# Load and fold steps of x, the order of S1 and S2, and the setup's order in a Fourier-filter-and-MLP kernel

## The chip, the cores and the metric

The kernel runs on one core of a Trainium2 chip. The metric is the device time of one execution in microseconds (us). TensorE is called PE, its weight loads PEld, VectorE is DVE, ScalarE is ACT, GpSimd is POOL or Pool, SyncE is SP; "SPq" is a transfer issued by SyncE. "Granted clock" is TensorE's clock as the profile records it, as a share of full speed.

## The reference

```python
def _attn_ref(x, filt_r, filt_i):            # x: (8, 3072, 256)
    X = np.fft.rfft(x, axis=1)
    Y = X * (filt_r + 1j * filt_i)[None, :, :]
    return np.fft.irfft(Y, n=x.shape[1], axis=1).astype(np.float32)

def _moe_ref(x, w1, w2, w_out):              # x: (24576, 256), w1, w2: (256, 1024)
    return (np.maximum(x @ w1, x @ w2) @ w_out).astype(np.float32)
```

A filter in the frequency domain along the sequence, then a maxout MLP. The FFTs are done as matmuls in stages: S1 (x times a cosine table), S2 and the multiply by the filter, S3, S4.

The names in the profiles: x lands as `xf` and is folded into `xd` (sum and difference of its halves), which S1 reads. S1's result `pa` is copied to `at`, written to DRAM as `ad` and read back as `bt` for S2 (`px`); the multiply by the filter gives `pq`, S3 gives `pz`, copied to `zt`, written to DRAM as `zd` and read back as `zr` for S4 (`py`). `ph` and `po` belong to the MLP, `ot` is the output tile. The p-tiles lie in PSUM, the memory of the matmuls' results, until another engine copies them out. In the setup, "spreads" lay out the filter by matmuls and copies, T1 are transposes for batch 0, and dummy matmuls have results that nobody uses. A "hole" is a stretch of some microseconds in which PE stands.

## The kernel before

One main loop runs over 48 output tiles of 8 steps each. Each step has two matmuls into `ph` (`moe_h`) and five into `po` (`moe_o`); the S1, S2 and S3 work of later batches is hung on certain steps by a list ("plan"). Batch b's S2 and S3 are a generator with eight groups; S1 of batch b+1 rides in six of them. Transfers of x, `ad`, `bt`, `zd` and `zr` are issued by SyncE; output tiles are stored by Pool, which also folds x.

```python
    def load_p(b, c):                        # x as fp32, two transfers of 256 KB
        ...
        for m in range(2):
            ...
            nc.sync.dma_start(out=xb[b, c][64 * m:64 * m + 64], in_=...)

    def fold_x(b, c):                        # Pool: sum and difference
        xf = xb[b, c]
        xb[b, c] = xpool.tile([128, 2, 2 * D], BF16, tag="xb", name="xd")
        for i, op in enumerate((OP.add, OP.subtract)):
            G.tensor_tensor(xb[b, c][:, i], xf[:, 0], xf[:, 1], op)
...
        for j, g in enumerate((4, 5, 6, 7, 2, 3, 1, 0)):           # one group
            px = [ps.tile(...) for _ in range(2)]
            ...                                                    # S2: 8 matmuls into px
            for k in range(2):
                V.tensor_tensor(pq[k][0:FROWS], px[k]..., F[...], OP.mult)
            if b + 1 < B and j in (0, 1, 3, 4, 6, 7):
                f1_half(b + 1, (0, 1, 3, 4, 6, 7).index(j))        # S1 of the next batch
            ...                                                    # S3 of the group before
...
        if j % 4 == 3:                                             # in moe_o
            V.tensor_copy(ot[tt][:, n - 1:n + 1], po[tt])
        if j == 7 ...:
            G.dma_start(out=dst[:, 4 * i:4 * i + 4], in_=ot[tt])   # store, Pool's queue
...
    opool = ctx.enter_context(tc.tile_pool(name="opool", bufs=2))
```

Of the kernel before, what the change touches and what calls it, by code (L numbers as in the profile page):

```python
# [13 lines left out]
B = 8  # L14
# [15 lines left out]
def kernel(  # L30
# [26 lines left out]
    V, S, G, TE = nc.vector, nc.scalar, nc.gpsimd, nc.tensor  # L57
# [30 lines left out]
    def bank2(shape, dtype, name, tag=None):  # L88
        if tag is None:
            ring.append(ring.pop(0))  # L90
            tag = ring[-1]
        return p2.tile(shape, dtype, tag=tag, name=name)
# [27 lines left out]
    def expand_f(g, ri, E, sp=0):  # L120
        if E is V:
            pf = [p2.tile([128, 2, D], FP32, tag="px", name="pf", bufs=4) for _ in range(2)]
        else:
            p_ = bank2([128, 2, 2, D], FP32, "pf")
            pf = [p_[:, b] for b in range(2)]
        fs = Fs[ri]
        spin(pf[0].rearrange("p u d -> p (u d)"), sp)
        for b in range(2):
            for c in range(2):
                m = 4 * b + c  # L130
                TE.matmul(pf[b][64 * c:64 * c + 32], Sel[:, m], fs[:, 2 * g:2 * g + 2], start=True, stop=True)
                p0 = 64 * c + 32
                if g:
                    TE.matmul(pf[b][p0:p0 + 32], Sel[:, 7 - m], fs[:, 16 - 2 * g:14 - 2 * g:-1], start=True, stop=True)
                else:
                    TE.matmul(pf[b][p0:p0 + 32, 0], Sel[:, 7 - m + c], fs[:, 0], start=True, stop=True)
                    TE.matmul(pf[b][p0:p0 + 32, 1], Sel[:, 7 - m], fs[:, 15], start=True, stop=True)
        f_ = F[:, ri, :, 2 * g:2 * g + 2].rearrange("p b u d -> p b (u d)")
        if E is V:
            for b in range(2):  # L140
                V.tensor_copy(f_[:, b], pf[b].rearrange("p u d -> p (u d)"))
        else:
            evac(E, f_, p_.rearrange("p b u d -> p b (u d)"))
# [142 lines left out]
    def table_e(t1):  # L286
        V.tensor_scalar(t1, pid, 12.0, None, OP.is_equal)
        V.tensor_scalar(e0[:, 0:1], pid, 0.0, t1, OP.is_equal, OP.add)
        V.tensor_scalar(e0[:, 1:2], e0[:, 0:1], -1.0, 1.0, OP.mult, OP.add)
        V.tensor_scalar(e0[:, 0:1], e0[:, 0:1], -0.5, 1.0, OP.mult, OP.add)  # L290
# [45 lines left out]
    def spin(pd, n):  # L336
        for _ in range(n):
            TE.matmul(pd, Sp, Sp.rearrange("p (o x) -> p o x", o=1).to_broadcast([128, 4, 128]), start=True, stop=True)
# [65 lines left out]
    def f1_half(b, c):  # L404
        if c == 0:
            ad[b] = dram.tile([128, N2, D], BF16, tag="ad", name="ad")
        at = apool.tile([128, 4, D], BF16, tag="at", name="at")
        pa = [ps.tile([128, 2, D], FP32, tag="ps", name="pa") for _ in range(2)]
        for m, i in QUADS:
            TE.matmul(pa[m][64 * i:64 * i + 64], C1[64 * m:64 * m + 64, 64 * i:64 * i + 64],  # L410
                      xb[b, c][64 * m:64 * m + 64, i], start=True, stop=True)
        for m in range(2):
            S.activation(at[:, 2 * m:2 * m + 2], pa[m], AF.Copy)  # L413
        nc.sync.dma_start(out=ad[b][:, 4 * c:4 * c + 4], in_=at)
# [17 lines left out]
    def gen_f2(b):  # L432
        bt_ = bt[b]
        zd[b] = dram.tile([T, 96, D], BF16, tag="zd", name="zd")
        pend = []
        zt = None

        def s3(g, pq):
            nonlocal zt
            if zt is None:  # L440
                zt = zpool.tile([128, 2, 4, D], BF16, tag="zt", name="zt")
                made.clear()
            pz = [ps.tile([128, 2, D], FP32, tag="ps", name="pz") for _ in range(2)]
            for i in range(2):
                for ri, W in enumerate((VP, VQ)):
                    for c, k in QUADS:
                        TE.matmul(pz[c][64 * k:64 * k + 64, i], W[64 * c:64 * c + 56, 2 * g + i, k],  # L447
                                  pq[k][64 * c:64 * c + 56, ri, i], start=(ri == 0), stop=(ri == 1))
            o = 2 * (g % 2)
            for c in range(2):  # L450
                S.activation(zt[0:ROWS, c, o:o + 2], pz[c][0:ROWS], AF.Copy)  # L451
            made.append(g)
            if len(made) == 2:
                t0 = 8 * (g // 2)
                for k in range(2):
                    nc.sync.dma_start(out=zd[b][t0:t0 + 8, 48 * k:48 * k + 48].rearrange("t p d -> p t d"),
                                      in_=zt[64 * k:64 * k + 48].rearrange("p c u d -> p (c u) d"))
                zt = None

        made = []  # L460
        for j, g in enumerate((4, 5, 6, 7, 2, 3, 1, 0)):
            px = [ps.tile([128, 2, D], FP32, tag="ps", name="px") for _ in range(2)]
            for i in range(2):
                for k, c in QUADS:
                    t_ = 16 * i + 4 * (g // 2) + 2 * c + g % 2
                    TE.matmul(px[k][64 * c:64 * c + 64, i], U[64 * k:64 * k + 48, 4 * g + 2 * i + c],  # L466
                              bt_[64 * k:64 * k + 48, t_], start=True, stop=True)
            pq = []
            for k in range(2):
                pq.append(pqpool.tile([128, 2, 2, D], BF16, tag="pq", name="pq"))  # L470
                V.tensor_tensor(pq[k][0:FROWS],  # L471
                                px[k][0:FROWS].rearrange("p (o i) d -> p o i d", o=1).to_broadcast([FROWS, 2, 2, D]),
                                F[0:FROWS, :, k, 2 * g:2 * g + 2], OP.mult)
            if b + 1 < B and j in (0, 1, 3, 4, 6, 7):
                f1_half(b + 1, (0, 1, 3, 4, 6, 7).index(j))
            pend.append((g, pq))
            if len(pend) > 1:
                s3(*pend.pop(0))
            yield
        while pend:  # L480
            s3(*pend.pop(0))
        yield
# [15 lines left out]
    def first_t1(g, E):  # L498
        pt = p2.tile([128, 2, 2, D], BF16, tag="px", name="pt", bufs=4)
        t0 = 8 * (g // 2) + 2 * (g % 2)  # L500
        for c in range(2):
            for i in range(2):
                for dh in range(2):
                    TE.transpose(pt[:, c, i, 128 * dh:128 * dh + 128],
                                 At[:, 2 * dh:2 * dh + 2].rearrange("p b m t -> p t (b m)")[:, t0 + 4 * c + i], I128)
        o = bt[0][0:ROWS, 8 * (g // 2):8 * (g // 2) + 8].rearrange("p (c u) d -> p c u d", c=2)[:, :, 2 * (g % 2):2 * (g % 2) + 2]
        evac(E, o.rearrange("p c u d -> p c (u d)"), pt[0:ROWS].rearrange("p c u d -> p c (u d)"))

    def evac(E, out_, in_):
        if E is V:  # L510
            V.tensor_copy(out_, in_)
        else:
            S.activation(out_, in_, AF.Copy)
# [156 lines left out]
    load_f0()  # L670
    patch_f0()
    first_s1(5, S, 2)
    expand_f(1, 1, S)
    expand_f(6, 0, V)
    expand_f(7, 0, S, 2)
    first_t1(1, V)
    first_t1(2, V)
    table_e(t1)
    pend = []
    for n, g in enumerate(order):  # L680
# [41 lines left out]
    def plan(step, fn, *a):  # L722
        todo.setdefault(step, []).append((fn, a))

    def plan_x(n, steps):
        for c, s_ in enumerate(steps):
            plan(s_, load_p, n, c)
            plan(s_ + 5, fold_x, n, c)

    def plan_f2(n, steps, z1, z0):  # L730
        g = []
# [11 lines left out]
    def spaced(first, gap, count):  # L743
        return [first + int(gap * i) for i in range(count)]
# [4 lines left out]
        plan(int(0.6 * (c - 1)), f1, 1, c, (S, V)[c % 2])  # L749
    plan(6, f1_read, 1)  # L750
    plan_f2(1, spaced(17, 1.9, 9), 28, 34)
    plan_x(2, (5, 7, 8, 10, 11, 13))
    plan(36, f1_read, 2)
    plan_x(3, spaced(32, 3.5, 6))
    plan_f2(2, spaced(60, 2.5, 9), 74, 81)
    plan(83, f1_read, 3)
    plan_x(4, spaced(76, 3.5, 6))
    plan_f2(3, spaced(104, 3, 9), 121, 129)
    plan(130, f1_read, 4)
    plan_x(5, spaced(122, 3.5, 6))  # L760
    plan_f2(4, spaced(150, 3.3, 9), 168, 178)
    plan(179, f1_read, 5)
    for n in range(5, B):
        o = 48 * (n - 5)
        if n + 1 < B:
            plan_x(n + 1, spaced(168 + o, 3.5, 6))
            plan(227 + o, f1_read, n + 1)
        plan_f2(n, spaced(197 + o, 3.4, 9), 216 + o, 226 + o)

# [3 lines left out]
    for tt in range(6 * B + 1):  # L773
        b, i = divmod(tt, 6)
# [40 lines left out]
```

## Time and profile before

| | before |
|---|---|
| time, median of 2 runs | 579.49 us (578.09 to 580.88) |
| span of the profiled execution | 579.7 us |
| PE busy | 520.9 us, 90% |
| mean granted clock | 0.962 |
| chain that ended last | PE 62%, DMA 18%, ACT 5%, DVE 5% |

How to read it: PE is the bound wherever it has work, and the chain says that a fifth of the end's cause lies in transfers. Which transfers, and when, the page does not tell; the waits by engine and the equal stretches do. The prediction shows them. The DMA share of a stretch adds up the time of the packets that begin in it, over 16 engines, so it can pass 1.

### The profile page before, as it was taken

The numbers are of one execution on the slowest core, as the hardware profiler recorded it, in microseconds if no ns is written. First come the engines' busy times: TensorE is split into PE (matmuls) and PEld (weight loads), VectorE is DVE, ScalarE is ACT, GpSimd is POOL, SyncE is SP. The second block draws the span as 40 slices with busy tenths as digits, with TensorE's granted clock in tenths as the row PEclk, the third lists the DMA queues.
The fourth block names the chain that finished last, engine by engine and source line by source line (L and its number), as shares of the span: only waits on it lengthen the run. The fifth ranks groups of instructions, "written<-read, shape, count | busy, mean of one in ns | idle before, by whom it ended". The sixth has DMA issues, their size and how long they took to land.

```text
span 579.7 us, 12530 instructions
## 1 busy us (share of the span) xinstructions
PE 520.9 (90%) x5206; PEld 352.9 (61%) x5284; DVE 322.5 (56%) x437; ACT 337.2 (58%) x597; POOL 147.9 (26%) x168
## 2 busy tenths in 40 slices
PE   8898859995999969995999996999789999999997
PEld 3556536663566646673566763676456766677775
DVE  8887437431773446542775346745377368734442
ACT  7777538643686546853566563755456556655452
POOL 6681163126004070232405240051400000000000
PEclk9999979998799989998999997999979999999999
DMA  8982995898368954989449983789535873451102
GB/s 150 275 142 87 166 259 154 233 197 198 137 177 226 211 177 128 265 164 209 142 137 286 204 176 122 202 234 210 173 101 156 166 171 93 119 155 73 72 39 109
DMA packets 74093, 97.03 MB, mean 167 GB/s; under 512 B 5106, under 2 KB 49780, under 8 KB 73044
## 3 DMA queue, kind: packets, MB, share of 16 engines
q1 hardware_dynamic: 63012, 63.72, 49.6%
q0 software_dynamic: 11024, 32.51, 17.9%
q8 instruction: 41, 0.67, 0.5%
q14 instruction: 16, 0.13, 0.1%
HBM read 54.79 MB, written 47.19 MB: 176 GB/s over the span
## 4 chain that ended last, share of the span: by engine, by line
PE 62%; DMA 18%; ACT 5%; DVE 5%; SPq 4%; issue 3%; POOL 2%; POOLq 0%; DVEq 0%; ACTq 0%
PE po L620 22%; PE ph L595 20%; DMA xf<-in_x_dram 6%; DMA out_dram<-ot 5%; PE po L615 5%; SPq L423 3%; PE pz L447 3%; ACT at L413 3%; PE px L466 3%; DMA zd<-zt 2%; PE py L579 2%; POOL xd L402 2%; DVE pq L471 2%; DMA bt<-ad 2%; PE pa L410 2%
## 5 line engine op out<-in xcount | busy, mean ns | idle before, releaser
L600 ACT ACTIVATE gt<-ph 128x512 bf16<-128x512 f32 x308 | 181.6, 602 | 131.9 <-PE ph L595 131.3
L620 PE MATMUL po<-Wo,gt 128*128 128x256 bf16 x1536 | 234.5, 277 | 4.0 <-issue 0.7
L620 PEld LDWEIGHTS <-gt 128*128 128x128 bf16 x1536 | 152.6, 99 | 61.1 <-issue 3.3
L622 DVE COPY ot<-po 128x512 f32<-128x512 f32 x96 | 66.3, 690 | 156.2 <-PE po L620 106.2
L471 DVE TENSOR_TENSOR pq<-px,F 120x1024 bf16<-120x1024 f32 x112 | 131.7, 1219 | 30.6 <-PE px L466 29.7
L402 POOL TENSOR_TENSOR xd<-xf 128x512 bf16<-128x512 f32 x72 | 89.3, 1264 | 141.9 <-DMA xf<-in_x_dram 102.3
L627 POOL DMA_DIRECT2D out_dram<-ot x47 | 25.7, 548 | 271.8 <-DVE ot L622 271.8
L595 PEld LDWEIGHTS <-Wd 128*128 128x128 bf16 x768 | 71.5, 99 | 28.5 <-issue 19.8
L451 ACT ACTIVATE zt<-pz 112x512 bf16<-112x512 f32 x112 | 60.9, 600 | 26.1 <-PE pz L447 24.9
L413 ACT ACTIVATE at<-pa 128x512 bf16<-128x512 f32 x72 | 39.1, 595 | 57.8 <-PE pa L410 57.8
L598 DVE TENSOR_SCALAR gt<-ph 128x512 bf16<-128x512 f32 x76 | 52.2, 687 | 34.6 <-PE ph L595 23.8
L410 PE MATMUL pa<-xd,C 64*64 64x512 bf16 x144 | 17.5, 405 | 28.1 <-DVE pq L471 15.2
L447 PE MATMUL pz<-pq,VP 56*64 56x256 bf16 x448 | 31.7, 283 | 7.0 <-DVE pq L471 4.9
L579 PE MATMUL py<-G,zr 128*128 128x128 bf16 x384 | 29.9, 219 | 1.8 <-ACT at L413 1.0
L447 PE MATMUL pz<-pq,VQ 56*64 56x256 bf16 x448 | 30.7, 281 | 0.0
L579 PEld LDWEIGHTS <-zr 128*128 128x128 bf16 x384 | 25.3, 98 | 5.1 <-issue 3.3
L466 PE MATMUL px<-bt,U 48*64 48x256 bf16 x448 | 24.2, 281 | 1.0 <-DMA bt<-ad 1.0
L410 PEld LDWEIGHTS <-C 64*64 64x64 bf16 x144 | 5.0, 109 | 30.6 <-DVE pq L471 16.6
L447 PEld LDWEIGHTS <-VP 56*64 56x64 bf16 x448 | 15.6, 109 | 11.6 <-issue 6.8
L466 PEld LDWEIGHTS <-U 48*64 48x64 bf16 x448 | 8.6, 104 | 13.5 <-issue 13.2
L447 PEld LDWEIGHTS <-VQ 56*64 56x64 bf16 x448 | 14.7, 111 | 1.8
L529 DVE TENSOR_TENSOR pq<-px,F 120x1024 bf16<-120x1024 f32 x11 | 13.2, 1220 | 2.4 <-issue 1.1
(388 smaller groups left out, 604.6 us busy)
## 6 DMA issues: line engine op xcount, KB each, us to landing
out_dram<-ot POOLq DMA_DIRECT2D x47, 512.0 KB, 4.4
xf<-in_x_dram SPq DMA_DIRECT2D x72, 256.0 KB
ad<-at SPq DMA_DIRECT2D x42, 256.0 KB
bt<-ad SPq DMA_DIRECT2D x56, 192.0 KB
zd<-zt SPq DMA_DIRECT2D x56, 192.0 KB
zr<-zd SPq DMA_DIRECT2D x14, 768.0 KB
xb<-in_x_dram POOLq DMA_DIRECT2D x12, 256.0 KB, 10.1
wf<-in_moe_w_dram POOLq DMA_DIRECT2D x2, 1024.0 KB, 10.3
```

What stands on the lines that cost most here:

```text
L402: G.tensor_tensor(xb[b, c][:, i], xf[:, 0], xf[:, 1], op)
L413: S.activation(at[:, 2 * m:2 * m + 2], pa[m], AF.Copy)
L447: TE.matmul(pz[c][64 * k:64 * k + 64, i], W[64 * c:64 * c + 56, 2 * g + i, k], pq[k][64 * c:64 * c + 56, ri, i], start=(ri == 0), stop=(ri ...
L451: S.activation(zt[0:ROWS, c, o:o + 2], pz[c][0:ROWS], AF.Copy)
L466: TE.matmul(px[k][64 * c:64 * c + 64, i], U[64 * k:64 * k + 48, 4 * g + 2 * i + c], bt_[64 * k:64 * k + 48, t_], start=True, stop=True)
L471: V.tensor_tensor(pq[k][0:FROWS], px[k][0:FROWS].rearrange("p (o i) d -> p o i d", o=1).to_broadcast([FROWS, 2, 2, D]), F[0:FROWS, :, k, 2 ...
L579: TE.matmul(py[:, n], zr[b][:, 4 * i + n, 128 * dc:128 * dc + 128], G1, start=True, stop=True)
L595: TE.matmul(ph, Wd[:, dc, 128 * j:128 * j + 128], y_[:, dc].rearrange("p a b -> p (a b)"), start=(dc == 0), stop=(dc == 1))
L598: V.tensor_scalar(gt[tt][:, j], ph, 0.0, None, OP.max)
L600: S.activation(gt[tt][:, j], ph, AF.Relu)
L620: TE.matmul(p_, g_[:, jj, 128 * n:128 * n + 128], Wo[:, jj], start=False, stop=(jj == 7))
L622: V.tensor_copy(ot[tt][:, n - 1:n + 1], po[tt])
```

## The change

Intent: let Pool find x landed when it comes to fold it, so that it never stands; and take S1's result out of PSUM earlier. The description speaks of x going through Pool's queue, but the diff leaves the loads on SyncE.

```diff
         made = []
+        units = (2, 3, 4, 5, 6, 7) if b == 1 else (0, 1, 3, 4, 6, 7)
         for j, g in enumerate((4, 5, 6, 7, 2, 3, 1, 0)):
+            if b + 1 < B and j in units:
+                f1_half(b + 1, units.index(j))
             px = [ps.tile([128, 2, D], FP32, tag="ps", name="px") for _ in range(2)]
...
-            if b + 1 < B and j in (0, 1, 3, 4, 6, 7):
-                f1_half(b + 1, (0, 1, 3, 4, 6, 7).index(j))
...
-    expand_f(1, 1, S)
     expand_f(6, 0, V)
-    expand_f(7, 0, S, 2)
     first_t1(1, V)
     first_t1(2, V)
+    expand_f(1, 1, S)
+    expand_f(7, 0, S)
...
-    def plan_x(n, steps):
+    def plan_x(n, steps, lag=12):
         for c, s_ in enumerate(steps):
             plan(s_, load_p, n, c)
-            plan(s_ + 5, fold_x, n, c)
+            plan(s_ + lag, fold_x, n, c)
...
-    plan_x(2, (5, 7, 8, 10, 11, 13))
+    plan_x(2, (5, 7, 8, 10, 11, 13), 6)
-    plan_x(3, spaced(32, 3.5, 6))
+    plan_x(3, spaced(24, 3, 6))
-    plan_x(4, spaced(76, 3.5, 6))
+    plan_x(4, spaced(64, 3.5, 6))
-    plan_x(5, spaced(122, 3.5, 6))
+    plan_x(5, spaced(108, 3.5, 6))
-            plan_x(n + 1, spaced(168 + o, 3.5, 6))
+            plan_x(n + 1, spaced(155 + o, 3.5, 6))
```

## The prediction

> **What bounds the kernel now.** I read the page's busy shares first, then the waits of each engine, then equal stretches of 8 us, then the timeline around one bad stretch. TensorE (PE) is busy 520.9 of 579.7 us, and no other engine passes 58%, so the other 59 us of PE are what a reordering can win. The 40 slices of the page show that they are not spread out: slices 6, 10, 15, 19, 25 and 29 (counted from 1) are at 5 to 7 tenths and most others at 9. The 8 us stretches sharpen that. Columns: stretch, PE busy (instructions), PEld, DVE, ACT, POOL, granted clock, DMA share, GB/s.
>
> ```profile
> 128.00:136.00 8.00, 8.00 (x70) 5.36 (x68) 2.07 (x4) 4.09 (x8) 1.89 (x2) 1.00 1.13 203
> 136.00:144.00 8.00, 2.62 (x23) 1.51 (x22) 0.71 (x2) 2.16 (x5) 7.25 (x8) 0.81 0.75 203
> 144.00:152.00 8.00, 6.09 (x37) 3.30 (x39) 5.80 (x6) 3.34 (x7) 2.29 (x4) 0.55 0.29 114
> 152.00:160.00 8.00, 7.69 (x99) 5.21 (x99) 5.96 (x6) 6.59 (x13) 0.00 (x0) 1.00 0.43 136
> ...
> 528.00:536.00 8.00, 7.95 (x64) 5.80 (x63) 3.23 (x5) 3.92 (x8) 0.53 (x1) 1.00 0.17 68
> ```
>
> PE works, stops for over 5 us, then works at about half the clock, then goes on. Stretches of this kind lie at 72, 136, 208, 264, 344 and 416 us: six, once for each of the batches 2 to 7 whose x is loaded and folded inside the loop. The last pass of the frequency stage (from about 470 us) has no fold beside it and has no hole. The waits by engine say who is the holder (columns: total us, times, longest us; the lines are from the answers for all engines and for DVE):
>
> ```profile
> POOL xd L402 <- DMA xf<-in_x_dram: 102.3, 12, 17.4
> DVE ot L622 <- DMA out_dram<-ot: 49.7, 6, 11.1
> PE pa L410 <- DVE pq L471: 15.2, 5, 6.4
> PE pa L410 <- POOL xd L402: 7.0, 2, 6.4
> ```
>
> VectorE (DVE) waits six times, 8.3 us each, for an output store to land. The timeline around 136 us gives the order:
>
> ```profile
> 134.11 2.50 POOL L402 TENSOR_TENSOR xd<-xf 128x512 bf16<-128x512 f32 x2 [10.44 <-DMA xf<-in_x_dram]
> ...
> 136.56 0.56 POOL L627 DMA_DIRECT2D out_dram<-ot  x1
> ...
> 143.29 0.69 DVE L622 COPY ot<-po 128x512 f32<-128x512 f32 x1 [11.09 <-DMA out_dram<-ot]
> 143.90 2.35 DVE L471 TENSOR_TENSOR pq<-px,F 120x1024 bf16<-120x1024 f32 x2
> 145.17 0.13 PEld L410 LDWEIGHTS <-C 64*64 64x64 bf16 x3 [6.66 <-DVE pq L471]
> ```
>
> Pool stood 10.44 us at a fold whose x had not landed. The store of a finished output tile sits behind that fold in Pool's order, so it is issued only at 136.56. The output tiles have two buffers; DVE waits for the store, and behind that wait stands the multiply that frees the PSUM buffer of the next matmul. So **a late load of x stops PE through a store that has nothing to do with x.** Only the first hole (72 us) is plainer: there PE waits 6.38 us for the fold itself.
>
> **What the Trainium skill says.** "TensorE: Matmul & The Clock Gate", Part 1: the array is at half clock after an idle window of about 3.4 us and comes back after a busy one. The trace agrees: the granted clock is at 0.5 in six spells, five of 6.83 us and one of 10.24 us (two and three such windows), each begun in one of the six holes or within half a microsecond of its end. The same page, Part 2, on queue depths, calls the queues of ScalarE, VectorE and GpSimd strict FIFO; the store behind the fold and the multiply behind the copy are that. "DMA: Bandwidth & Descriptors", section on issuing engines, says that transfers from all issuers run on the same 16 DMA engines and interleave. The trace agrees: the spells with most traffic (share 1.13 to 1.22) are those where the loads of x, the reads of bt and of zr, and stores overlap, and there a load of x took 9 to 10 us from issue to landing.
>
> **The change part by part.** The short description speaks of Pool's queue, but the diff leaves the loads of x on the SyncE queue; I go by the diff.
>
> To measure in the program's own clock I count the matmuls of L620, eight to two steps of the main loop, and take the time of the first of each eight. Two steps take 2.0 us outside the frequency stage and 3.3 us with one group of it.
>
> 1. *Folds 12 steps behind loads instead of 5; loads 8 to 14 steps earlier.* The folds keep about their places (those of batch 3: steps 36 to 51, were 37 to 54), so the load gains the time. 5 steps are 5 to 7 us, less than a load under traffic (9 to 10 us); 12 steps are 12 to 17 us, more than it. It also takes most loads ahead of the bt reads (steps 83, 130, 179, 227), behind which SyncE now issues them; eight such reads took 8.52 us to issue before batch 7. Now the holes, each as the time of its two steps less 3.3 us: step 62: 12.89, so 9.6; step 110: 10.33, so 7.0; step 150: 10.70, so 7.4; step 206: 10.26, so 7.0; step 254: 10.56, so 7.3. Sum 38.3 us for batches 3 to 7, with most of the half-clock loss in it. I take all of it off.
> 2. *Batch 2: S1 at groups 2 to 7 instead of 0, 1, 3, 4, 6, 7, folds 6 steps behind.* The first hole is step 18: 12.65, so 9.3 us. Its loads can't come earlier: five of six wait behind the bt reads (issued 66.7 to 77.1 us), and the folds end at 64.6, 79.1, 82.8, and then about 85.8, 88.3 and 90.8. Moving S1 back gives PE two groups and two steps to do meanwhile. Going on from 70 us at the usual pace, the six S1 would fall at about 75, 78.4, 82.5, 86, 89 and 92.6: only the second and third would still wait, 0.7 and 0.3 us, too short to lose the clock. I leave 2 us: gain 7.3.
> 3. *S1 ahead of S2 in each group.* No work added or removed. S1's result leaves PSUM 0.4 us earlier (the length of S2's 8 matmuls). PE waited 5.3 us in 21 places, up to 0.3 us each, for the copies of S1 (L413). I count 2 us of it.
> 4. *Setup: T1 ahead of the last spreads, two dummy matmuls gone.* T1 starts at 20.85 us behind a spread and two dummies (0.61 us as shown), but DVE is still copying the last spread until 20.95. I count 0.4 us.
> 5. *Half clock beyond the holes' own steps.* The spells reach 0.3 to 2.6 us past them (219.2 to 219.5, 356.9 to 359.5), 6.7 us in all; half of it: 3 us.
>
> Sum: 38.3 + 7.3 + 2 + 0.4 + 3 = 51 us, so **528.5 us** with every hole closed. Cross-check: the batch without a fold took 57.4 us (465.6 to 523.0, 48 steps); adding six S1 of 0.4 us gives 59.8 us, where the four between 96 and 288 took 67.7, 69.3, 68.1 and 68.4: 8.6 each above it. That is 34 us for four, and some 17 for the two earlier: 51 as well. Against it I set 4 us for waits that come up once the holes are gone (next part). **Prediction: 532 us.**
>
> **The rivals.**
>
> *The DMA engines become the bound.* Between 136 and 416 us their share averages 0.76 and peaks at 1.22. The same bytes in batches of 60 instead of 69 us make 0.87. For: that is near the peaks, and loads took 9 to 10 us there. Against: the peaks came from bunching, the group stretches stood at 0.3 to 0.5, and exactly there the new loads go. If it did bind at a few places, holes of 2 to 4 us in three batches: 540 to 545.
>
> *Another wait on SyncE's queue.* Loads now stand between the writes of ad and zd, and SyncE takes them in order. The read of zr waits for zd to land (19 waits, up to 4.2 us), and PE needs zr 12 or 13 steps after the last group. In batch 1 zr came by about 118.6 us and was used at about 121. Loads ahead of it could make a wait of 1 to 2 us in each batch, up to 10 us: 542. Against: loads that used to share this very window now precede it.
>
> *The fold slot still too early.* If loads land later than 12 steps, Pool blocks as before but for less; each microsecond past the slack of the two output buffers goes to PE. With half of the holes left, some 555.
>
> *A hidden move.* If PE were bound otherwise, the time would stay. The batch without folds at 57.4 us speaks against it.
>
> **Range and chances.** Below lies the floor of 528 less perhaps 4 us for what point 3 might give beyond my count; above, one rival coming true. 80%: 524 to 545. Within 2% would need over 568, that is four of six holes left: 3%. Slower: 1%.
>
> **What would show it.** Right: waits of Pool for xf from 102 us to under 30, DVE's waits for the output store from 49.7 to under 8; PE busy at 96% or more of the span with a mean clock of 0.98 or better; two-step times never over about 6 us in the groups; no wait over 3 us on PE after the setup. Step 2 wrong: a wait over 3 us on S1 in batch 2, near 75 to 85 us. A rival right: PE waiting at L579 (zr) or at L466 (bt) in every batch, or Pool's waits for xf still near 10 us. The prediction is wrong if the half-clock spells stay, or if the loads, now inside the groups, delay ad, zd or the output stores so that new holes open at other steps.

## The result and the profile after

The changed kernel took 525.63 us (525.53 to 525.73, 2 runs), before 579.49 us: ratio 0.9071, 95% interval 0.8976 to 0.9165. A repeat with more runs gave 527.92 us (526.51 to 529.62, 6 runs) beside 579.4 us: ratio 0.9118, 0.9092 to 0.9144. Ratios are the mean time of one kernel's fast runs over that of the other's of the same rounds, so they are not quite the ratio of the medians.

Line numbers move by one to three: L620, L471 and L622 of before are L621, L474 and L623 in the changed kernel. First the equal stretches of the changed kernel that hold the same work as those shown of before (columns as there):

```profile
120.00:128.00 8.00, 8.00 (x71) 5.46 (x69) 2.98 (x5) 4.21 (x8) 2.59 (x3) 1.00 0.80 197
128.00:136.00 8.00, 7.89 (x96) 5.25 (x95) 6.85 (x8) 6.58 (x13) 3.42 (x4) 1.00 0.64 212
136.00:144.00 8.00, 7.82 (x101) 5.42 (x101) 6.27 (x7) 7.25 (x15) 0.00 (x0) 1.00 0.69 201
144.00:152.00 8.00, 7.86 (x100) 5.46 (x100) 6.88 (x8) 6.73 (x15) 3.03 (x3) 1.00 0.92 264
```

PE goes on at full clock through the groups of batch 2, which begin at about 127 us here and began at 134.8 us before. The DMA share in the groups is higher (0.64 to 0.92, where before 0.29 to 0.43 stood behind the hole), because the loads of the next x now lie there. Next the waits of Pool and DVE in the changed kernel (total us, times, longest us):

```profile
POOL xd L402 <- DMA xf<-in_x_dram: 46.2, 4, 17.1
POOL out_dram L628 <- DMA xf<-in_x_dram: 9.8, 2, 7.8
DVE ot L623 <- DMA out_dram<-ot: 1.3, 1, 1.3
```

Pool's waits for x at the folds fell from 102.3 to 46.2 us, and DVE's for a store from 49.7 to 1.3 us. A store can still stand behind a late fold: the fold at 125.41 us waited 11.19 us, and the store behind it went out at 130.32 us. But DVE took its next output tile at 137.16 us without a wait, so nothing was lost. PE's own waits are all small now; the three longest:

```profile
PE pd L338 <- DVE Sp L167: 1.1, 1, 1.1
PE px L469 <- DMA bt<-ad: 1.0, 2, 0.6
PE pf L131 <- DMA Fs<-in_filt_r_dram: 0.9, 1, 0.9
```

The chain that ended last, by engine, has no transfer in it any more:

```profile
PE 76%; issue 1%; DVE 1%; ACT 0%
```

The same comparison in the program's own clock: the time of the first of each eight matmuls into `po`, eight to two steps, gives the length of any stretch of steps.

| steps | before, us | changed, us | gained, us |
|---|---|---|---|
| 8 to 48 | 63.8 | 56.6 | 7.2 |
| 48 to 96 | 69.9 | 58.8 | 11.1 |
| 96 to 144 | 67.7 | 59.1 | 8.6 |
| 144 to 192 | 69.3 | 59.3 | 10.0 |
| 192 to 240 | 68.1 | 59.1 | 9.1 |
| 240 to 288 | 68.4 | 59.1 | 9.3 |
| 288 to 336 (groups, but no fold and no S1) | 57.4 | 57.4 | 0.0 |
| 336 to 384 (no group) | 48.7 | 48.7 | 0.0 |

The last two rows are a control that the kernel brings with it: where no x is folded and no S1 is done, nothing changed. The gains sum to 55.3 us, and the setup gave 0.7 more (step 8 came at 57.7 instead of 58.4 us).

### The profile page after: what moved, and what is told of

Read it like the earlier page. It is cut to its first block, busy times and chain, and to the rows that moved or that the text cites. A ratio compares the mean times of both kernels' runs of the same rounds, so it can differ in the third digit from the quotient of the medians.

```text
span 523.8 us, 12526 instructions
## 1 busy us (share of the span) xinstructions
PE 504.0 (96%) x5204; PEld 346.5 (66%) x5282; DVE 322.4 (62%) x437; ACT 336.9 (64%) x597; POOL 148.0 (28%) x168
## 4 chain that ended last, share of the span: by engine, by line
PE 76%; issue 1%; DVE 1%; ACT 0%
PE po L621 30%; PE ph L596 26%; PE po L616 7%; PE pz L447 4%; PE py L580 3%; PE px L469 2%; PE pa L410 2%; DVE pq L474 0%; ACT at L413 0%; DVE ot L623 0%
## 5 line engine op out<-in xcount | busy, mean ns | idle before, releaser
L621 PE MATMUL po<-Wo,gt 128*128 128x256 bf16 x1536 | 229.8, 273 | 3.4
L621 PEld LDWEIGHTS <-gt 128*128 128x128 bf16 x1536 | 150.2, 98 | 57.6
L474 DVE TENSOR_TENSOR pq<-px,F 120x1024 bf16<-120x1024 f32 x112 | 131.7, 1219 | 32.6 <-PE px L469 32.4
L623 DVE COPY ot<-po 128x512 f32<-128x512 f32 x96 | 66.2, 690 | 103.9 <-PE po L621 102.3
L402 POOL TENSOR_TENSOR xd<-xf 128x512 bf16<-128x512 f32 x72 | 89.1, 1268 | 47.2 <-DMA xf<-in_x_dram 46.2
L451 ACT ACTIVATE zt<-pz 112x512 bf16<-112x512 f32 x112 | 61.0, 602 | 19.5 <-PE pz L447 16.4
L447 PE MATMUL pz<-pq,VP 56*64 56x256 bf16 x448 | 29.4, 271 | 1.1 <-DVE pq L474 0.8
L447 PE MATMUL pz<-pq,VQ 56*64 56x256 bf16 x448 | 28.6, 268 | 0.0
L469 PEld LDWEIGHTS <-U 48*64 48x64 bf16 x448 | 11.6, 106 | 9.2 <-issue 6.0
L447 PEld LDWEIGHTS <-VP 56*64 56x64 bf16 x448 | 14.1, 105 | 3.7 <-issue 2.4
L410 PE MATMUL pa<-xd,C 64*64 64x512 bf16 x144 | 15.2, 400 | 0.0
L514 ACT ACTIVATE F<-pf 128x1024 bf16<-128x1024 f32 x10 | 10.1, 1032 | 6.7 <-PE pf L134 6.7
## 6 DMA issues: line engine op xcount, KB each, us to landing
xb<-in_x_dram POOLq DMA_DIRECT2D x12, 256.0 KB, 10.6
wf<-in_moe_w_dram POOLq DMA_DIRECT2D x2, 1024.0 KB, 10.3
```

The source lines that it names most:

```text
L447: TE.matmul(pz[c][64 * k:64 * k + 64, i], W[64 * c:64 * c + 56, 2 * g + i, k], pq[k][64 * c:64 * c + 56, ri, i], start=(ri == 0), stop=(ri ...
L451: S.activation(zt[0:ROWS, c, o:o + 2], pz[c][0:ROWS], AF.Copy)
L469: TE.matmul(px[k][64 * c:64 * c + 64, i], U[64 * k:64 * k + 48, 4 * g + 2 * i + c], bt_[64 * k:64 * k + 48, t_], start=True, stop=True)
L474: V.tensor_tensor(pq[k][0:FROWS], px[k][0:FROWS].rearrange("p (o i) d -> p o i d", o=1).to_broadcast([FROWS, 2, 2, D]), F[0:FROWS, :, k, 2 ...
L621: TE.matmul(p_, g_[:, jj, 128 * n:128 * n + 128], Wo[:, jj], start=False, stop=(jj == 7))
```

## The experiments

Twelve kernels ran, all of them correct; before took 580.0 us beside runs 1 to 4, 580.72 beside 5 to 8 and 579.4 beside 9 to 12.

**1. The plan alone:** the kernel before with the load and fold steps of batches 3 to 7.

```diff
-            plan(s_ + 5, fold_x, n, c)
+            plan(s_ + lag, fold_x, n, c)           # lag = 12; batch 2 keeps 5
-    plan_x(3, spaced(32, 3.5, 6))
+    plan_x(3, spaced(24, 3, 6))                    # and batches 4 to 7 as in the change
```

> The kernel before with the load and fold steps of batches 3 to 7 alone (loads earlier, folds 12 steps behind); batch 2, the order of S1 and S2 and the setup as before. Theory (late folds hold back the output stores, and these hold DVE and PE): the five holes at steps 62, 110, 150, 206 and 254 close, two-step times there fall from 10.3-12.9 to about 3.3 us, the first hole (step 18, 12.65 us) stays; 579.5 less 38 to 45 is 535 to 542 us. Rival (the order of S1 ahead of S2 closes the holes): they stay, and the time is over 565 us.

Measured: 540.55 us (538.27 to 542.21), ratio 0.9326. The two-step times at the five holes fell from 12.9, 10.3, 10.7, 10.3 and 10.6 to 3.4, 2.8, 2.6, 3.4 and 3.4 us; step 18 stayed, at 13.4. Pool's waits for x at the folds are 47.8 us here, and DVE waits for no store. So the plan is worth 39.5 us, and the order of S1 and S2 is not what closes these five.

**2. Batch 2 alone.**

```diff
-            if b + 1 < B and j in (0, 1, 3, 4, 6, 7):
+            if b + 1 < B and j in ((2, 3, 4, 5, 6, 7) if b == 1 else (0, 1, 3, 4, 6, 7)):
...
-    plan_x(2, (5, 7, 8, 10, 11, 13))
+    plan_x(2, (5, 7, 8, 10, 11, 13), 6)
```

> The kernel before with S1 of batch 2 in groups 2 to 7 and its folds 6 steps behind, nothing else. Theory: the first hole (step 18) shrinks from 12.65 to about 4 us, the five others stay; 579.5 less 7 to 9 is 570 to 573 us. Rival (the first hole is given back later, at the next late fold): 576 to 580 us.

Measured: 577.21 us (576.09 to 577.58), ratio 0.9955 (0.9898 to 1.0012). A miss: 2.8 us instead of 7 to 9, within the rival's range. The two steps at 18 fell only to 5.6 us; steps 8 to 48 took 59.6 us, 4.2 less than before (56.6 in the changed kernel); and the next hole grew from 12.9 to 13.8. With S2 still first, PE waits for DVE at S1 seven times in this kernel, where it did five times before:

```profile
PE pa L410 <- DVE pq L471: 17.7, 7, 7.3
```

**3. The order of S1 and S2 alone.**

```diff
         for j, g in enumerate((4, 5, 6, 7, 2, 3, 1, 0)):
+            if b + 1 < B and j in (0, 1, 3, 4, 6, 7):
+                f1_half(b + 1, (0, 1, 3, 4, 6, 7).index(j))
...
-            if b + 1 < B and j in (0, 1, 3, 4, 6, 7):
-                f1_half(b + 1, (0, 1, 3, 4, 6, 7).index(j))
```

> The kernel before with S1 ahead of S2 in each group, at the same groups, nothing else. Theory: the holes stay, since the stores are as late as before; only the waits of up to 0.3 us for the copies of S1 (5.3 us in all) go: 574 to 579 us. Rival (order frees the PSUM buffers on which PE stands in the holes): under 560 us.

Measured: 573.19 us (571.61 to 574.43), ratio 0.9891. All six holes stay, so the rival falls; but the gain of 6.8 us is just over what I gave it. It is not in batch 2: steps 8 to 48 took 64.5 us, 0.7 more than before. The holes of the later batches are shorter (the two steps at 206 and 254 took 8.7 and 8.3 us instead of 10.3 and 10.6), and the half-clock spells there lasted 3.4 instead of 6.8 us.

**4. A third output buffer, with folds and loads as late as before.** This takes away what makes DVE wait for a late store. To make room, the S1 copies have three buffers instead of five.

```diff
-    apool = ctx.enter_context(tc.tile_pool(name="apool", bufs=5))
+    apool = ctx.enter_context(tc.tile_pool(name="apool", bufs=3))
...
-    opool = ctx.enter_context(tc.tile_pool(name="opool", bufs=2))
+    opool = ctx.enter_context(tc.tile_pool(name="opool", bufs=3))
```

> The kernel before with three buffers for output tiles instead of two (and three instead of five for the S1 copies, to make room), nothing else: folds and loads stay as late as they were. Theory: Pool waits for x as long as before (about 100 us), but the late stores stop nobody, DVE's waits for a store (49.7 us) fall under 10, and the holes of batches 3 to 7 close or shrink to under 2 us each: 540 to 552 us. Rival (PE stands for the folds themselves, and the store is only in the same place): the holes stay, now as waits of PE for a fold, and the time is over 565 us.

Measured: 539.75 us (539.19 to 539.94), ratio 0.9314, the same as the plan alone: the two kernels' stretches of steps from 48 on agree to 0.1 us in every row. Yet Pool waited at the folds nearly as long as before, while DVE's waits for a store are gone from its list. First the wait, then the timeline at the place of the hole shown of before, then the equal stretches there, all of this kernel:

```profile
POOL xd L402 <- DMA xf<-in_x_dram: 88.9, 14, 17.9
```

```profile
135.13 2.50 POOL L402 TENSOR_TENSOR xd<-xf 128x512 bf16<-128x512 f32 x2 [10.18 <-DMA xf<-in_x_dram]
137.57 0.56 POOL L627 DMA_DIRECT2D out_dram<-ot  x1
```

```profile
136.00:144.00 8.00, 7.50 (x88) 4.85 (x91) 5.94 (x7) 6.58 (x13) 7.60 (x8) 1.00 0.98 268
144.00:152.00 8.00, 7.69 (x106) 5.34 (x111) 5.95 (x6) 6.30 (x13) 3.03 (x4) 1.00 0.63 182
```

The fold waits 10.18 us and the store is issued at 137.57 us, as late as before (136.56), and PE does not stop. So in batches 3 to 7 the folds themselves were in time for S1; what stopped PE was the store behind them together with the second output buffer. The first hole stays (12.9 us at step 18): there PE waits for the fold itself.

**5 and 6. The lag alone, and the loads alone.**

```diff
-            plan(s_ + 5, fold_x, n, c)             # run 5: loads at their old steps,
+            plan(s_ + lag, fold_x, n, c)           #        lag = 12 (batch 2: 5)
...
-    plan_x(3, spaced(32, 3.5, 6))                  # run 6: loads at the new steps (so for
+    plan_x(3, spaced(24, 3, 6))                    #        batches 3 to 7), lag 5 as before
```

> The kernel before with the folds of batches 3 to 7 at 12 steps behind their loads instead of 5; the loads stay at their old steps, so the folds come 7 steps later. Theory (what counts is that a fold finds its x landed when Pool reaches it): Pool's waits for x fall from 102 us to 40-60, DVE's waits for stores under 10, all five holes close: 537 to 545 us, as with loads and lag together (540.6). Rival (the loads must move too, since the bt reads ahead of them on SyncE's queue take 8.5 us to issue and the load then takes 9 to 10): holes of 2 to 5 us stay in most batches, 550 to 565 us.

> The kernel before with the loads of batches 3 to 7 at the changed kernel's earlier steps and folds 5 steps behind as before, so the folds come earlier too. Theory: inside the groups five steps last about 7 to 8 us and there is less traffic, so most loads land in time or nearly so, and a fold that waits 2 or 3 us stays within the slack of the two output buffers: 538 to 548 us. Rival (the lag is what does it): stores are held back by each fold as before, holes of 3 us and over remain: over 555 us.

Measured: the lag alone 539.82 us (538.74 to 541.01), ratio 0.9297; the loads alone 553.87 us (552.19 to 554.35), ratio 0.9538. The lag alone does all that the plan does: every stretch of steps from 48 on is that of run 1 to 0.1 us, and DVE waits for no store, though Pool waits 63.4 us for x (just over the forecast). With the loads alone the holes of the last three batches closed too, but two stayed (the two steps at 62 took 10.2 us, and steps 96 to 144 took 66.8). DVE's waits for a store in run 6:

```profile
DVE ot L622 <- DMA out_dram<-ot: 17.8, 2, 9.4
```

Neither side of that forecast was right as a whole. Both holes have the first mechanism's order in the timelines. Pool folds at 134.54 us and issues two stores at 139.43 us, and DVE waits for one until 142.58 us; the loads of those folds were issued only from 123.91 us, behind eight bt reads. Again Pool folds at 191.40 us, from a load issued at 183.19 us, and issues two stores at 193.83 us, and DVE waits 9.43 us until 202.57 us. That these folds stood for x is inferred from the times of issue: the profile puts their waits down to PE.

**7. S2 first again, in the changed kernel.**

```diff
-            if b + 1 < B and j in units:
-                f1_half(b + 1, units.index(j))
             px = [ps.tile([128, 2, D], FP32, tag="ps", name="px") for _ in range(2)]
...
+            if b + 1 < B and j in units:
+                f1_half(b + 1, units.index(j))
             pend.append((g, pq))
```

> The changed kernel with S2 put back ahead of S1 in each group, all else as changed. From the run of the plan alone, batches 3 to 7 took 60.0 us against 59.1 in the changed kernel, with 25 waits of up to 0.3 us for the copies of S1; so theory: 5 us over six batches, plus up to 2 in batch 2, where S1 of late folds stands behind S2: 530 to 533 us against 525.6. Rival (the order is worth nothing once the holes are closed, the 0.9 us has another source): within 1 us of 525.6.

Measured: 536.72 us (535.61 to 541.06), ratio 0.9261, where the changed kernel had 0.9071 and 0.9118: some 9 to 11 us more by the medians, about twice the forecast. In the profiled execution (the slowest of four, 541.06 us) the stretches from step 96 to 288 took 60.0 to 60.3 us instead of 59.1 to 59.3, as expected, but steps 8 to 48 took 65.3 instead of 56.6, and 48 to 96 took 61.9 instead of 58.8. PE's longest waits in this kernel show why:

```profile
PE ph L596 <- ACT at L413: 6.3, 25, 0.3
PE py L580 <- DMA zr<-zd: 4.5, 1, 4.5
PE pa L410 <- DVE pq L472: 2.1, 2, 1.3
```

The first and third are the order's own price. The second is new: in batch 1, whose groups are the densest of the kernel (1.9 steps apart), the groups end later, the last writes of zd and the read of zr come later, and PE stands for zr at step 46. A half-clock spell of 6.8 us follows. How much of the zr wait the three faster executions had is not on record.

**8. The setup's old order, in the changed kernel.**

```diff
+    expand_f(1, 1, S)
     expand_f(6, 0, V)
+    expand_f(7, 0, S, 2)
     first_t1(1, V)
     first_t1(2, V)
-    expand_f(1, 1, S)
-    expand_f(7, 0, S)
```

> The changed kernel with the setup's old order (T1 behind the last spreads, two dummy matmuls back). Theory: the first step of the main loop comes 0.4 to 0.8 us later, nothing else moves: 526.0 to 526.5 us. Rival: the setup's end is bound by other waits, no difference, 525.6.

Measured: 529.48 us (526.36 to 531.34), ratio 0.9117. Step 8 came at 58.5 us instead of 57.7 (57.7 to 58.0 in all profiles with the new setup), and T1 began at 20.93 us instead of 18.69. The rest of the 3.9 us to the first runs of the changed kernel can't be laid to the setup: the profiled execution waits 2.1 us for zr, and the repeat of the changed kernel (run 9) has the same ratio. What is shown is 0.8 us at the loop's start.

**9 and 10. The changed kernel once more, and with the loads of batch 3 later.**

```diff
-    plan_x(3, spaced(24, 3, 6))                    # run 10 only
+    plan_x(3, spaced(35, 3, 6))
```

> The changed kernel once more, as the yardstick for the three runs beside it and to see its spread: two variants of it showed waits of 2.1 and 4.5 us for zr of batch 1 near step 46. Theory: that wait is on the edge in the changed kernel too, so some executions show it: median 526 to 528 us, spread 2 us or more. Rival: it has slack here, all runs within 1 us of 525.6.

> The changed kernel with the loads of batch 3 eleven steps later (35 to 50 instead of 24 to 39, folds still 12 behind), so that four of them no longer stand ahead of the reads of zr of batch 1 or share the DMA engines with the writes of zd. Theory: zr comes 2 to 5 us earlier relative to its use, no execution waits for it: 524 to 526 us, and a spread under 1 us. Rival (zr's edge comes from the group spacing, not from the loads): as the repeat beside it, or worse because the loads now meet the bt reads.

Measured: the repeat 527.92 us (526.51 to 529.62, 6 runs), ratio 0.9118; with the later loads 525.9 us (525.41 to 526.43, 5 runs), ratio 0.9084 (0.9059 to 0.9109). The profiled execution of the repeat waits for zr:

```profile
PE py L580 <- DMA zr<-zd: 1.1, 1, 1.1
```

That of run 10 shows no such wait, and SyncE issued its second read of zr at 104.24 us instead of 106.06, which is 2.3 us earlier against its own step 46. So the changed kernel stands on an edge in batch 1, and taking four loads away from it gives the kernel 2 us under the repeat and with a third of its spread (1.0 us, just over the forecast). The margin is narrow: the two intervals overlap a little, and the two first runs of the changed kernel were as fast.

**11. Batch 2 as before, in the changed kernel.**

```diff
-        units = (2, 3, 4, 5, 6, 7) if b == 1 else (0, 1, 3, 4, 6, 7)
+        units = (0, 1, 3, 4, 6, 7)
...
-    plan_x(2, (5, 7, 8, 10, 11, 13), 6)
+    plan_x(2, (5, 7, 8, 10, 11, 13), 5)
```

> The changed kernel with batch 2 as before: S1 in groups 0, 1, 3, 4, 6, 7 and folds 5 steps behind. Theory: the first hole comes back at step 18 with about 7 us of standing and a half-clock spell: 532 to 535 us. Rival (the order of S1 and S2 already cured part of it): 528 to 531 us.

Measured: 533.41 us (532.19 to 534.45), ratio 0.9212, 5.5 us over the repeat. The two steps at 18 take 13.7 us again, with a half-clock spell of 10.2 us, and PE waits for the fold itself, as before:

```profile
77.93 0.58 PE L410 MATMUL pa<-xd,C 64*64 64x512 bf16 x1 [7.11 <-POOL xd L402]
```

With runs 2 and 3 the profiles say that this part is worth more with the order. In steps 8 to 48 it gained 4.2 us alone and 6.8 with S1 first (64.3 in this run against 57.5 in the repeat), while the order alone gained nothing there. The medians (2.8 us alone, 5.5 with S1 first) differ in the same sense, but within their intervals.

**12. The groups of batch 1 one step later as well.**

```diff
-    plan_f2(1, spaced(17, 1.9, 9), 28, 34)
+    plan_f2(1, spaced(18, 1.9, 9), 29, 35)
-    plan_x(3, spaced(24, 3, 6))
+    plan_x(3, spaced(36, 3, 6))
```

> As the run with later loads of batch 3 (here 36 to 51), and the frequency stage of batch 1 one step later (18 instead of 17), so that its first S2 finds bt landed (1.0 us of waits for bt and 0.8 for the multiply behind it). Theory: 1 us less than the run with later loads alone. Rival: the last groups and with them zd and zr also come one step later, and PE waits for zr: 1 to 3 us more.

Measured: 530.69 us (529.87 to 533.43), ratio 0.9175. It lost 5 us against run 10 instead of gaining one, and not through zr. Waits of PE and of DVE in this kernel:

```profile
PE py L580 <- DVE pq L474: 3.8, 2, 3.1
DVE ot L623 <- DMA out_dram<-ot: 5.1, 2, 3.8
```

Up to step 28 it was 1.4 us ahead of the repeat (86.41 and 87.84 us), so the first half of the theory held. Then DVE waits 3.78 us, until 88.32 us, for a store that Pool issued at 81.14 us behind a fold; the multiply behind that copy holds PE for 3.1 us, and a half-clock spell of 6.8 us follows. The store itself was no later than in the repeat (issued at 81.79 us, awaited 1.1 us until 89.23): one group less stood ahead of the copy, so DVE came to it 3.6 us earlier. So the store behind the late folds of batch 2, with their short lag of 6 steps, leaves no slack there either.

## Why the prediction was right

The prediction was 532 us, from 528.5 with every hole closed; measured were 525.6 and 527.9. In the two profiles the sum can be closed by stretches of steps, 56.0 us of gain in all: 43.1 from the plan (run 1 against before, steps 48 to 288), 5.0 more in the same steps from run 1 to the changed kernel, 7.2 in steps 8 to 48, and 0.7 in the setup. The prediction had 41.3, 2, 7.3 and 0.4, less 4.

- **What bounds the kernel.** Right, and run 4 shows it apart from the plan: with a third output buffer the folds are as late as before and five holes are gone. Of DVE's six waits for a store, five (8.4 to 11.1 us) end in these five holes; the sixth (2.86 us at 126.8 us) comes before them, and the first hole has none.
- **Points 1 and 5, the plan and its half clock, 41.3 us.** Measured alone 39.5 us. PE's standing in the five holes of before is 6.35 and 0.69, 4.20 and 0.71, 5.92, 3.53 and 0.73, 3.84 and 0.73, together 26.7 us; run 1 gained 43.1 us over the five stretches from step 48 to 288 (9.8, 7.7, 9.0, 8.2 and 8.4). By an estimate, the 16.4 us between are for the most part work at half clock in the holes' wake: the five spells last 37.6 us together (one of 10.24, four of 6.83), about 30 of them after PE had started again, and half of that is 15 (successive L620 matmuls start 213 ns apart in the spells, 109 ns outside, by the medians). The reason given was too wide, though: of "folds later behind their loads" and "loads earlier", the first alone does it (run 5), and the second alone leaves two holes (run 6).
- **Point 2, batch 2, 7.3 us.** Steps 8 to 48 gained 7.2 us. That the part would do so by itself was wrong: alone it gained 4.2 there (run 2), so the close match has some luck in it.
- **Point 3, the order, 2 us.** This is the term that was mis-sized: 5.0 us in steps 48 to 288 alone, some 9 to 11 us in the changed kernel (run 7, the stand for zr included), 6.8 in the kernel before (run 3, where it mainly shortened holes). I counted a part of the 5.3 us of PE's waits for S1's copies. All 21 of those are gone from the list of waits, and beyond them the order takes time out of the dense groups of batch 1, where a delay runs on into zd, zr and S4.
- **Point 4, the setup, 0.4 us.** Measured 0.7 to 0.8 us at the loop's start.
- **The allowance of 4 us for new waits.** Too large for the first runs, whose profiled execution has no wait of PE over 1.1 us. The rival behind it, zr, is real but only in batch 1: 1.1, 2.1 and 4.5 us in the profiles of the repeat and of two variants. The rival of busy DMA engines did not come true: the share in the groups rose, and yet in the changed kernel PE's only waits on transfers are 1.0 us for bt of batch 1 and 0.9 us in the setup.
- **The signs.** One failed: Pool's waits for x were to fall under 30 us and are 46.2, the longest 17.1, which stood there as a sign of a rival. The other signs came (DVE's waits for a store 1.3 us, PE 96% busy at a mean clock of 0.999, no half-clock spell before 523.1 us, no wait of PE over 1.1 us). Pool's waits are the wrong sign: run 4 has 88.9 us of them and no store waited for.
- **The cross-check.** Its 17 us for the two earlier batches were assumed, not read; measured were 18.3, and 37.0 for the four others, where it had 34.

The time came out 4 to 6 us too high because the order was undercounted and the allowance overcounted. The parts measured singly (39.5, 2.8, 6.8 and 0.8 us) make 49.9, against 51.5 to 53.9 for the whole, a difference within their intervals.

## What to carry to other kernels

Here a queue that held both computation and stores handed the waits of the computation on to the stores; look for a store that is issued late, not only for an engine that waits, and count the buffers between it and the engine that sets the time. Placing a consumer well behind its load cost nothing here and was worth more (40.9 us) than issuing the load earlier (26.9 us). A hole in PE's work costs more than its length: 27 us of standing came with some 16 us more, by the estimate above most of it work at half clock.

## What the Trainium skill lacked or had wrong

- "TensorE: Matmul & The Clock Gate", Part 1, ties the half clock in its table to an idle window of about 3.4 us; a section further on ("A second HAM failure mode") has it from short idle times between groups of matmuls too, but without a figure. In run 10 a spell of 3.41 us at half clock began at 71.9 us, after a window in which PE was busy for 1.95 us of 3.40 and no wait was longer than 0.9 us (columns as before). In all fourteen profiles the clock changes on a grid of 3.413 us. By this grid, each of the 27 windows at full clock with at most 1.35 us of PE busy was followed by half clock, 5 of the 12 with 1.6 to 2.01 us, and none of the 2080 with more (PE's busy time by the profile, where the ends of matmuls are modelled).

```profile
68.50:71.90 3.40, 1.95 (x23) 0.95 (x18) 2.30 (x3) 0.60 (x1) 0.00 (x0) 1.00 1.25 175
71.90:75.30 3.40, 3.29 (x23) 1.75 (x24) 2.47 (x4) 1.57 (x3) 0.00 (x0) 0.50 1.10 220
```

- "DMA: Bandwidth & Descriptors", section on issuing engines, calls the sequencer's time to start a transfer usually small relative to the transfer. For one transfer that holds: 1.05 us beside the 9 to 10 us of a load of x from issue to landing. What the page does not say is that it can double in one kernel: in the changed one eight bt reads took SyncE 3.94 us from 62.03 us (DMA share 0.80 meanwhile) and 8.52 us from 106.09 us (share 0.98), and ten loads of x 10.50 us, and what stands behind them starts that much later.
- "GPSIMD Engine Reference", section on performance pitfalls, lists costs per element and per command, but not that a store issued from Pool's queue stands behind a Pool computation that waits for its data; that had to be inferred from the strict FIFO queues of the TensorE page. Here that was worth 40 us of 580 (runs 1, 4 and 5).
